# Chunked attention and a phase MLP on one core: zero products at the start, a token mix in three parts, and late transposes moved to DMA

## The chip, the cores and the metric

The kernel runs on one core of one Trainium2 chip. The core has TensorE (PE, matrix products; its weight loads are listed as PEld), VectorE (DVE), ScalarE (ACT), GpSimd (POOL) and SyncE (SP), which run at the same time and wait for each other by semaphores. DMA engines move data between HBM and SBUF and inside SBUF. The metric is the device time of one execution in microseconds (us), taken as the median of several runs. The span, a little shorter, is the time from the first to the last instruction in a profiled execution.

## What is computed

Inputs q, k, v have the shape (8 batches, 8 heads, 576 tokens, 64). Attention works inside chunks of 64 tokens; its result x (8, 576, 512) goes through a layer that turns each value by a phase, mixes the tokens and mixes the channels:

```python
# attention, per batch, head and chunk of 64 tokens
scores = scale * q_c @ k_c.T
attn = softmax(scores)
x = attn @ v_c                       # heads laid side by side: (8, 576, 512)
# phase layer
theta = x @ w_theta
zr, zi = x * cos(theta), x * sin(theta)
y = w_tok_r @ zr + w_tok_i @ zi      # over the 576 tokens of a batch
u = x + y
out = u + max(u @ w_ch, 0)           # (8, 576, 512), float32
```

## The kernel before

The batches are taken in four pairs (0 to 3). The 2 x 576 tokens of a pair are nine tiles of 128 rows, numbered 0 to 8: tiles 0 to 3 belong to the first batch, 5 to 8 to the second, and tile 4, the middle tile, holds the last 64 tokens of both. For attention the tiles form five groups: A (0, 1), B (2, 3), M (4), C (5, 6), D (7, 8).

The whole program is a list of steps in ORDER. A step such as `Y.31.1` is a kind (Y), a pair (3), a tile or group (1), and for TensorE's steps a number of the PSUM buffer. Each engine does its own steps in the order of the list. The start and the end of the list before:

```python
ORDER = """
lw.00 init.00 cw.00 q.0B TW.00.0 q.0A q.0M k.0B k.0A twd.00 T.0B.1 tk.0B lt.00 twa.00
T.0A.2 tq.0B tk.0A tq.0A S.0B.1 k.0M v.0A v.0M v.0B e.0B S.0A.0 e.0A T.0M.2 tq.0M tk.0M
new.00 q.0D q.1M S.0M.1 lw.01 V0.0A.2 e.0M V0.0M.0 v0.0A v0.0M q.0C V1.0M.1 v1.0M
V1.0A.2 X.0M.0 k.1M v1.0A k.0D k.0C V1.0B.1 v.0D q.1A v1.0B X.0A.2 lc.00 x.0M H.0M.0
V0.0B.1 x.0A q.2M v0.0B g.0M H.0A.2 X.0B.1 z.0M TW.01.0 twd.01 x.0B new.10 H.0B.1 v.1M
g.0A z.0A TW.02.2 twd.02 g.0B twa.01 z.0B T.0D.1 twa.02 tq.0D T.0C.0 T.1M.2 tk.1M Y.02.0
... cut ...
H.3C.1 U.30.0 u.30 W.28.1 w.28 W.30.0 w.30 W.31.1 w.31 g.3C z.3C W.32.0 Y.33.1 w.32 y.33
Y.37.0 Y.34.1 y.37 y.34 U.37.0 u.37 U.33.1 u.33 U.34.0 W.37.1 w.37 u.34 Y.36.0 W.34.1
y.36 w.34 W.33.0 w.33 Y.35.1 y.35 U.36.0 U.35.1 u.36 W.36.0 u.35 w.36 Y.38.1 y.38 W.35.0
U.38.1 w.35 u.38 W.38.0 w.38
""".split()
```

The kinds, as far as they matter here: q, k, v load inputs (issued by GpSimd, cast to 16 bit on the way); lw, lt, lc load the weights and cw casts one of them; TW turns the token weights on TensorE, twd and twa copy them out of PSUM on DVE and ACT; T, tq, tk turn q and k; S, e, V0, V1, v0, v1 are attention (scores, exponential, product with v, division). Then follow, for a group or a tile:

```python
    # X, x: x turned by TensorE, copied out by ACT
    def x_t(p, g, slot):
        j0, bb, s0 = GROUPS[g]
        n = 1 if bb is None else 2
        ps = psum2("ps_xT", slot, FP16)
        psv = ps.rearrange("p (r x) -> p r x", r=2)[:, :, 0 : n * NDB * CH]
        psv = psv.rearrange("p r (a c) -> p r a c", c=CH)
        for j in range(n):
            for db in range(NDB):
                for r in range(2):
                    nc.tensor.transpose(
                        psv[:, r, j * NDB + db, :],
                        st[p]["x"][half[r], j0 + j, db * P : db * P + P],
                        id16[half[r], half[r]],
                    )
        st[p]["ps_xT", g] = psv
    def x_copy(p, g):
        n = 1 if g == "M" else 2
        psv = st[p].pop(("ps_xT", g))
        xT = tmp.tile([P, 2 * NDB, P], FP16, name="xT")
        st[p]["xT", g] = xT
        nc.scalar.copy(
            out=xT[:, 0 : n * NDB].rearrange("p a (r c) -> p r a c", r=2), in_=psv
        )

    # H: theta = x @ w_theta (8 products for two tiles); g: cos and sin on ACT
    # z: zr and zi; the middle tile's halves for the other batch's rows move by DMA
    def phase(p, g):
        j0, bb, s0 = GROUPS[g]
        cos, sin = st[p].pop(("trig", g))
        x, zr, zi = st[p]["x"], st[p]["zr"], st[p]["zi"]
        if bb is not None:
            nc.vector.tensor_mul(zr[:, j0 : j0 + 2], x[:, j0 : j0 + 2], cos)
            nc.vector.tensor_mul(zi[:, j0 : j0 + 2], x[:, j0 : j0 + 2], sin)
            return
        lo, hi = half
        t = tmp.tile([P, DM], FP16, name="zmid")
        nc.vector.tensor_mul(t[lo], x[lo, j0], sin[lo, 0])
        nc.vector.tensor_mul(t[hi], x[hi, j0], cos[hi, 0])
        nc.sync.dma_start(zr[hi, j0], t[lo])
        nc.sync.dma_start(zi[lo, j0], t[hi])
        nc.vector.tensor_mul(zr[lo, j0], x[lo, j0], cos[lo, 0])
        nc.vector.tensor_mul(zi[hi, j0], x[hi, j0], sin[hi, 0])

    # Y: token mix of one tile, nine products (middle tile: two of half width each)
    def y(p, j, slot):
        s = st[p]
        ps = psum1("ps_y", slot)

        if j == MID:
            parts = [(half[bb], slice(KT * P, S), bb) for bb in range(2)]
        else:
            bb = int(j > MID)
            jl = j - bb * (MID + 1)
            parts = [(slice(0, P), slice(jl * P, jl * P + P), bb)]
        for i in range(2 * KT + 1):
            for rows, cols, bb in parts:
                if i == 0:
                    z, jz, kt = s["zi"] if bb else s["zr"], MID, 2 * KT
                else:
                    kt = i - 1
                    z = s["zr"] if kt < KT else s["zi"]
                    jz = bb * (MID + 1) + kt % KT
                nc.tensor.matmul(
                    ps[rows], wT[:, kt, cols], z[:, jz, :],
                    start=(i == 0), stop=(i == 2 * KT),
                )
        s["ps_y", j] = ps

    # y: u = x + y
    def add_x(p, j):
        u = tmp.tile([P, DM], FP16, name="u16", bufs=6)
        st[p]["u", j] = u
        nc.vector.tensor_tensor(
            out=u, in0=st[p].pop(("ps_y", j)), in1=st[p]["x"][:, j], op=ALU.add
        )

    # U, u: u turned by TensorE, copied out by DVE or ACT
    def u_t(p, j, slot):
        u = st[p]["u", j]
        ps = psum1("ps_uT", slot, FP16)
        psv = ps[:, 0:DM]
        for db in range(NDB):
            nc.tensor.transpose(
                psv[:, db * P : db * P + P], u[:, db * P : db * P + P], id16
            )
        st[p]["ps_uT", j] = psv

    def u_copy(p, j):
        uT = tmp.tile([P, DM], FP16, name="uT", bufs=4)
        st[p]["uT", j] = uT
        psv = st[p].pop(("ps_uT", j))
        if j % 2:
            nc.vector.tensor_copy(out=uT, in_=psv)
        else:
            nc.scalar.copy(out=uT, in_=psv)

    # W: u @ w_ch, four products; w: the last add, and the stores
    def w(p, j, slot):
        uT = st[p].pop(("uT", j))
        ps = psum1("ps_uw", slot)
        for db in range(NDB):
            nc.tensor.matmul(
                ps, uT[:, db * P : db * P + P], wch16[:, db, :],
                start=(db == 0), stop=(db == NDB - 1),
            )
        st[p]["ps_uw", j] = ps
    def relu_add(p, j):
        u = st[p].pop(("u", j))
        o = outp.tile([P, DM], FP32, name="o32")
        nc.vector.scalar_tensor_tensor(
            out=o, in0=st[p].pop(("ps_uw", j)), scalar=0.0, in1=u, op0=ALU.max, op1=ALU.add
        )
        if j == MID:
            to = [out[2 * p + b, KT * P : S, :] for b in range(2)]
        else:
            bb = int(j > MID)
            jl = j - bb * (MID + 1)
            s0 = (jl // 2) * GT + (jl % 2) * CH
            to = [out[2 * p + bb, s0 + r * P : s0 + r * P + CH, :] for r in range(2)]
        for r in range(2):
            nc.sync.dma_start(to[r], o[half[r]])
```

PSUM has buffers of two sizes, "wide" (three are used, by T, S, V, X, H, TW) and "thin" (two, by Y, U, W).

Of the kernel before, what the change touches and what calls it, by code (L numbers as in the profile page):

```python
# [18 lines left out]
lw.00 init.00 cw.00 q.0B TW.00.0 q.0A q.0M k.0B k.0A twd.00 T.0B.1 tk.0B lt.00 twa.00  # L19
T.0A.2 tq.0B tk.0A tq.0A S.0B.1 k.0M v.0A v.0M v.0B e.0B S.0A.0 e.0A T.0M.2 tq.0M tk.0M  # L20
new.00 q.0D q.1M S.0M.1 lw.01 V0.0A.2 e.0M V0.0M.0 v0.0A v0.0M q.0C V1.0M.1 v1.0M
V1.0A.2 X.0M.0 k.1M v1.0A k.0D k.0C V1.0B.1 v.0D q.1A v1.0B X.0A.2 lc.00 x.0M H.0M.0
V0.0B.1 x.0A q.2M v0.0B g.0M H.0A.2 X.0B.1 z.0M TW.01.0 twd.01 x.0B new.10 H.0B.1 v.1M
g.0A z.0A TW.02.2 twd.02 g.0B twa.01 z.0B T.0D.1 twa.02 tq.0D T.0C.0 T.1M.2 tk.1M Y.02.0
tk.0D S.0D.1 tq.1M q.1D S.1M.2 tk.0C y.02 e.0D Y.00.1 tq.0C k.1A y.00 Y.01.0 y.01 e.1M
U.00.1 v.0C V0.0D.0 v0.0D V1.0D.1 u.00 V0.1M.2 U.02.0 v1.0D W.00.1 v0.1M S.0C.0 w.00
q.1B X.0D.1 u.02 V1.1M.2 W.02.0 w.02 x.0D v1.1M H.0D.1 U.01.1 e.0C V0.0C.0 V1.0C.2 v0.0C
Y.03.0 k.1D v1.0C g.0D q.1C X.0C.0 T.1A.2 u.01 T.1D.1 x.0C y.03 tq.1A tq.1D k.1B v.1B
H.0C.0 U.03.1 tk.1D W.01.0 v.1C z.0D tk.1A X.1M.1 u.03 W.03.1 w.01 g.0C k.1C S.1D.2 z.0C
T.1B.0 tq.1B k.2M w.03 q.2B x.1M e.1D S.1A.1 Y.05.0 y.05 v.1A e.1A tk.1B Y.06.1 T.1C.2  # L30
S.1B.1 q.2D T.2M.0 q.2A y.06 tq.1C v.1D Y.08.0 tk.2M U.05.1 tk.1C e.1B tq.2M V0.1A.2
u.05 S.2M.0 e.2M y.08 S.1C.1 W.05.1 V1.1B.0 q.2C v0.1A U.08.0 v1.1B H.1M.2 e.1C V0.1B.1
V1.1A.0 u.08 v1.1A v0.1B w.05 Y.04.0 g.1M q.3C v.2M V1.1C.0 X.1B.1 y.04 v1.1C V0.1C.2
U.06.1 v0.1C Y.07.0 y.07 u.06 U.04.1 V0.1D.0 k.2D v0.1D V1.1D.2 x.1B v1.1D X.1A.1 W.08.0
k.2C w.08 v.2B H.1B.0 v.3M u.04 U.07.1 u.07 x.1A new.20 W.06.0 w.06 k.2B v.3C W.04.1
V0.2M.1 g.1B X.1C.2 x.1C X.1D.0 W.07.0 w.04 w.07 q.3A H.1A.2 k.2A v0.2M x.1D H.1D.0 z.1M
z.1B q.3D H.1C.1 v.3B g.1A T.2D.2 g.1D V1.2M.0 z.1A Y.10.1 Y.11.0 tq.2D tk.2D v1.2M g.1C
y.10 U.10.1 z.1D X.2M.2 T.2B.0 S.2D.1 v.2D y.11 z.1C x.2M tq.2B T.2A.2 Y.13.0 tk.2B
tq.2A y.13 H.2M.0 v.2C q.3M k.3C u.10 U.11.1 tk.2A u.11 W.10.0 w.10 g.2M e.2D z.2M
Y.15.1 T.2C.2 tk.2C S.2B.0 y.15 e.2B tq.2C V0.2D.1 v.2A v0.2D Y.12.0 y.12 U.15.1 S.2A.2  # L40
e.2A u.15 S.2C.1 V1.2D.0 U.13.0 v.3A u.13 e.2C W.11.1 Y.16.0 V1.2A.2 V0.2A.1 w.11 v1.2D
X.2D.0 U.12.1 y.16 u.12 W.13.0 W.15.1 v1.2A w.13 U.16.0 x.2D v0.2A H.2D.2 w.15 v.3D
W.12.1 w.12 V1.2B.0 V0.2C.1 u.16 v0.2C g.2D v1.2B Y.14.0 y.14 k.3A V1.2C.1 X.2A.0 x.2A
v1.2C V0.2B.2 Y.18.1 U.14.0 v0.2B T.3A.1 z.2D u.14 X.2C.0 X.2B.2 y.18 W.16.0 w.16 x.2C
H.2A.0 Y.17.1 y.17 x.2B tq.3A H.2C.2 W.14.0 k.3D g.2A U.17.1 g.2C w.14 H.2B.0 k.3M u.17
z.2C W.17.0 q.3B k.3B tk.3A T.3M.2 w.17 tk.3M S.3A.1 g.2B U.18.1 Y.27.0 tq.3M z.2B
T.3C.0 e.3A T.3D.2 V0.3A.1 y.27 z.2A u.18 W.18.0 tk.3C tq.3C new.30 w.18 Y.25.1 S.3M.0
tq.3D tk.3D v0.3A e.3M S.3D.2 e.3D T.3B.1 y.25 V1.3A.0 U.27.0 v1.3A u.27 tq.3B tk.3B
Y.26.1 y.26 W.27.0 U.25.1 S.3B.2 V1.3M.0 V0.3M.1 w.27 u.25 v1.3M Y.24.0 X.3A.0 v0.3M
e.3B y.24 V1.3B.2 V1.3D.1 U.26.1 Y.22.0 y.22 u.26 W.26.1 w.26 x.3A Y.21.0 X.3M.0 v1.3B  # L50
y.21 V0.3B.2 W.25.1 x.3M U.22.0 v1.3D H.3M.0 u.22 Y.23.0 v0.3B w.25 g.3M y.23 Y.20.1
U.23.0 S.3C.1 X.3B.2 x.3B V0.3D.0 u.23 W.22.0 y.20 w.22 W.23.1 U.20.0 H.3B.2 e.3C z.3M
v0.3D lw.00 H.3A.1 u.20 w.23 g.3B U.21.0 u.21 g.3A W.20.1 w.20 Y.28.0 z.3B y.28 U.24.1
z.3A V1.3C.0 X.3D.2 V0.3C.1 u.24 U.28.0 u.28 W.24.1 w.24 W.21.0 v1.3C v0.3C w.21 x.3D
Y.31.1 X.3C.2 y.31 H.3D.0 U.31.0 g.3D u.31 x.3C Y.32.1 y.32 Y.30.0 U.32.1 z.3D y.30 u.32
H.3C.1 U.30.0 u.30 W.28.1 w.28 W.30.0 w.30 W.31.1 w.31 g.3C z.3C W.32.0 Y.33.1 w.32 y.33
Y.37.0 Y.34.1 y.37 y.34 U.37.0 u.37 U.33.1 u.33 U.34.0 W.37.1 w.37 u.34 Y.36.0 W.34.1
y.36 w.34 W.33.0 w.33 Y.35.1 y.35 U.36.0 U.35.1 u.36 W.36.0 u.35 w.36 Y.38.1 y.38 W.35.0
U.38.1 w.35 u.38 W.38.0 w.38
# [4 lines left out]
def kernel(  # L64
# [35 lines left out]
    VP = D + 2  # L100
    half = [slice(0, CH), slice(CH, P)]
# [27 lines left out]
    wnat = glob.tile([P, KT + 1, 2, S], FP16, name="wnat")  # L129
    wraw = pairp.tile([P, KT, S], FP32, name="wraw")  # L130
    wend = glob.tile([CH, S], FP32, name="wend")
    v16 = glob.tile([P, 2 * NT, H, VP], FP16, name="v16")

    def setup():
        make_identity(nc, id16)
        nc.vector.memset(pihalf, math.pi / 2.0)
        nc.vector.memset(v16[:, :, :, D : D + 1], 1.0)
# [267 lines left out]

    def y(p, j, slot):
        s = st[p]
        ps = psum1("ps_y", slot)  # L410

# [143 lines left out]
```

The softmax here doesn't subtract the row's maximum and nothing guards it: scores larger than these inputs give would overflow.

## Time and profile before

| | before |
|---|---|
| device time, median of 3 runs | 221.02 us (220.84 to 221.03) |
| span of the profiled execution | 216.8 us |
| TensorE busy | 189.2 us (87%), 2898 products |
| DVE busy | 126.6 us (58%) |
| ACT busy | 119.0 us (55%) |
| GpSimd busy (issuing the input loads) | 104.3 us (48%) |

A line of the profile names the line of the kernel (L426), the engine, the operation and the tiles that it writes and reads. In a line of waits, the engine and line that waited stand first, then what it waited for, the time in total, how often, and the longest. In the chain of what ended last, each piece has a start, a length and what ran, or what was waited for. GpSimd's issues are the input loads: they run from 1.4 us to about 117 us, after that the DMA engines carry only the output stores and the small moves of the middle tile.

### The profile page before, as it was taken

To read this page: it belongs to the slowest core of one execution; us is meant where nothing else is said; L and a number is where in the kernel's file an instruction comes from. 1 tells how busy PE (TensorE), PEld (TensorE's weight loads), DVE (VectorE), ACT (ScalarE), POOL (GpSimd) and SP (SyncE) were. 2 spreads that over 40 slices of the span, in tenths; PEclk is the share of its full clock that TensorE was granted. 3 is DMA by queue.
4 is the path that set the end of the run, shared out by engine and by line. 5 is a ranking of instruction groups with operands and counts; after the bars stand their busy time and mean duration, and the time that the engine had idled before them with its cause. 6 is when DMAs were issued, how large, how long until landed. Compare 5 with 4: busy or idle time off the path is not lost.

```text
span 216.8 us, 6577 instructions
## 1 busy us (share of the span) xinstructions
PE 189.2 (87%) x2898; PEld 101.0 (47%) x2898; DVE 126.6 (58%) x248; ACT 119.0 (55%) x133; POOL 104.3 (48%) x130
## 2 busy tenths in 40 slices
PE   0354798999999999759999999989999999998881
PEld 0243445554555554426554554555455454444430
DVE  0024546576856876818776936877465794564541
ACT  2435359837895657844947476943266945501110
POOL 8998888799999899869982000000000000000000
PEclk9999999999999999999999999999999999999998
DMA  6999999999999999999999420322040772080534
GB/s 200 179 166 157 161 162 166 176 146 181 182 184 187 154 182 186 235 163 152 155 176 205 116 51 19 81 53 49 5 92 16 205 238 62 3 194 0 120 74 97
DMA packets 121819, 28.90 MB, mean 133 GB/s; under 512 B 113920, under 2 KB 116032, under 8 KB 121792
## 3 DMA queue, kind: packets, MB, share of 16 engines
q0 software_dynamic: 114176, 15.88, 112.1%
q1 hardware_dynamic: 7616, 12.62, 21.7%
q8 instruction: 22, 0.36, 0.7%
q14 instruction: 5, 0.04, 0.1%
HBM read 34.39 MB, written 9.44 MB: 202 GB/s over the span
## 4 chain that ended last, share of the span: by engine, by line
PE 70%; ACT 8%; DMA 7%; POOL 6%; DVE 5%; issue 1%; POOLq 0%; ACTq 0%
PE ps_y L426 30%; PE ps_uw L462 13%; PE ps_theta L365 13%; POOL qk L160 5%; PE ps_uT L444 4%; DMA v<-in_v_dram 4%; DMA zr<-zmid 3%; PE ps_x L309 3%; PE ps_xT L340 2%; PE ps_qkT L245 2%; PE ps_sT L276 2%; ACT cos L381 2%; DVE x L322 2%; ACT sin L385 2%; ACT kT L263 1%
## 5 line engine op out<-in xcount | busy, mean ns | idle before, releaser
L426 PEld LDWEIGHTS <-wT 128*128 128x128 f16 (+1 forms) x360 | 30.9, 100 | 38.2 <-DMA zr<-zmid 3.5
L426 PE MATMUL ps_y<-zr,wT 128*128 128x512 f16 (+1 forms) x180 | 41.4, 380 | 3.4 <-DMA zr<-zmid 3.4
L426 PE MATMUL ps_y<-zi,wT 128*128 128x512 f16 (+1 forms) x180 | 44.3, 380 | 0.0
L435 DVE TENSOR_TENSOR u<-ps_y,x 128x512 f16<-128x512 f32 x36 | 24.8, 690 | 30.2 <-PE ps_y L426 29.9
L462 PE MATMUL ps_uw<-wch,uT 128*128 128x512 f16 x144 | 35.9, 380 | 0.9 <-ACT uT L456 0.7
L365 PE MATMUL ps_theta<-wtheta,xT 128*128 128x512 f16 x144 | 36.3, 399 | 0.3 <-ACT xT L352 0.3
L168 POOL DMA_DIRECT2D v<-in_v_dram x40 | 34.1, 876 | 4.7 <-DMA v<-in_v_dram 1.5
L160 POOL DMA_DIRECT2D qk<-in_k_dram x40 | 34.1, 886 | 3.3 <-DMA qk<-in_k_dram 0.8
L160 POOL DMA_DIRECT2D qk<-in_q_dram x40 | 34.3, 885 | 1.7 <-issue 0.6
L471 DVE SCALAR_TENSOR_TENSOR o<-ps_uw,u 128x512 f32<-128x512 f32 x36 | 24.8, 688 | 17.0 <-PE ps_uw L462 17.0
L456 ACT COPY uT<-ps_uT 128x512 f16<-128x512 f16 x20 | 11.7, 586 | 35.3 <-PE ps_uT L444 35.3
L352 ACT COPY xT<-ps_xT 128x1024 f16<-128x1024 f16 (+1 forms) x20 | 18.4, 930 | 21.3 <-PE ps_xT L340 21.2
L322 DVE TENSOR_TENSOR x<-ps_x,recip 128x512 f16<-128x512 f32 (+1 forms) x40 | 25.5, 638 | 1.4
L381 ACT ACTIVATE cos<-ps_theta,pihalf 128x1024 f16<-128x1024 f32 (+1 forms) x20 | 20.6, 1031 | 10.3 <-PE ps_theta L365 5.8
L263 ACT COPY kT<-ps_qkT 128x1024 f16<-128x1024 f16 x16 | 16.0, 1016 | 13.9 <-DVE qT L263 9.2
L365 PEld LDWEIGHTS <-xT 128*128 128x128 f16 x144 | 13.9, 101 | 16.5 <-issue 2.6
L289 ACT ACTIVATE eT<-ps_sT 128x1024 f16<-128x1024 f32 (+1 forms) x20 | 18.4, 939 | 4.2 <-PE ps_sT L276 4.0
L462 PEld LDWEIGHTS <-uT 128*128 128x128 f16 x144 | 12.7, 98 | 14.0 <-ACT uT L456 1.2
L385 ACT ACTIVATE sin<-ps_theta 128x1024 f16<-128x1024 f32 (+1 forms) x20 | 18.7, 936 | 0.0
L245 PE MATMUL ps_qkT<-id,qk 64*128 64x64 f16 x576 | 13.1, 197 | 2.8 <-DMA qk<-in_k_dram 2.0
L444 PE MATMUL ps_uT<-id,u 128*128 128x128 f16 x144 | 14.0, 220 | 1.1 <-DVE u L435 1.0
L263 DVE COPY qT<-ps_qkT 128x1024 f16<-128x1024 f16 x16 | 10.8, 686 | 5.4 <-ACT kT L263 4.7
(40 smaller groups left out, 151.6 us busy)
## 6 DMA issues: line engine op xcount, KB each, us to landing
out_dram<-o SPq DMA_DIRECT2D x72, 128.0 KB, 2.9
qk<-in_q_dram POOLq DMA_DIRECT2D x32, 128.0 KB, 6.5
qk<-in_k_dram POOLq DMA_DIRECT2D x32, 128.0 KB, 6.2
v<-in_v_dram POOLq DMA_DIRECT2D x32, 128.0 KB, 6.5
wraw<-in_moe_w_tok_r_dram SPq DMA_DIRECT2D x2, 1152.0 KB, 6.3
wnat<-in_moe_w_tok_i_dram POOLq DMA_DIRECT2D x1, 576.0 KB, 6.6
qk<-in_q_dram POOLq DMA_DIRECT2D x8, 64.0 KB, 6.3
wtheta<-in_moe_w_theta_dram POOLq DMA_DIRECT2D x1, 512.0 KB, 7.1
```

Source lines behind the costliest of these rows:

```text
L160: nc.gpsimd.dma_start(nats[p, g][rows, which, r], (q, k)[which][b, :, t0 : t0 + n, :].rearrange("h s d -> s h d"),)
L168: nc.gpsimd.dma_start(v16[rows, slot + r, :, 0:D], v[b, :, t0 : t0 + n, :].rearrange("h s d -> s h d"),)
L263: copy(out=t.rearrange(flat), in_=ps.rearrange(flat))
L322: nc.vector.tensor_tensor(out=st[p]["x"][:, j0 : j0 + n, f * NE * D : (f + 1) * NE * D].rearrange("p c (h d) -> p c h d", h=NE), in0=psv[: ...
L365: nc.tensor.matmul(ps[:, j * DM : j * DM + DM], xT[:, j * NDB + db, :], wtheta16[:, db, :], start=(db == 0), stop=(db == NDB - 1),)
L381: nc.scalar.activation(out=cos[:, 0:n].rearrange("p a e -> p (a e)"), in_=pin, func=AF.Sin, bias=pihalf, scale=1.0,)
L385: nc.scalar.activation(out=sin[:, 0:n].rearrange("p a e -> p (a e)"), in_=pin, func=AF.Sin)
L426: nc.tensor.matmul(ps[rows], wT[:, kt, cols], z[:, jz, :], start=(i == 0), stop=(i == 2 * KT),)
L435: nc.vector.tensor_tensor(out=u, in0=st[p].pop(("ps_y", j)), in1=st[p]["x"][:, j], op=ALU.add)
L444: nc.tensor.transpose(psv[:, db * P : db * P + P], u[:, db * P : db * P + P], id16)
L462: nc.tensor.matmul(ps, uT[:, db * P : db * P + P], wch16[:, db, :], start=(db == 0), stop=(db == NDB - 1),)
L471: nc.vector.scalar_tensor_tensor(out=o, in0=st[p].pop(("ps_uw", j)), scalar=0.0, in1=u, op0=ALU.max, op1=ALU.add)
```

## The change

The kernel after computes the same. Its differences:

1. **Products of zeros.** A new tile `blank` of zeros is filled at the start, and fourteen steps D are put between TensorE's first steps. Each is two products of 128x512 whose result nobody reads. They are there to keep the array active while it waits for its first inputs.
2. **The first token mix in three parts.** For the first four tiles of pair 0, Y is cut into Ya (products 0 and 1: zr of group A), Yb (4 and 5: zi of group A) and Yc (the rest), so that it can begin before all of z is there.
3. **The middle tile last.** Each Y now ends with the products of the middle tile instead of beginning with them, and the DMA that moves its halves is a step of its own (zm), apart from z.
4. **Late u and x by DMA transposes.** For the five groups of pair 3, and for twenty tiles of pairs 1 to 3, X and x, or U and u, give way to one DMA transpose (Xd, Ud), issued by SyncE, which writes the turned tile straight to SBUF.
5. **The store as a step of its own** (st), apart from the last add, so that the order of the DMAs on SyncE's queue can be chosen.
6. **A new order** of all steps, with group M first at the start. A second load of a token weight (lw.00), near the end of the old list and read by nothing, is gone.

The diff, cut to its core (of the ORDER list the start, the places of the first transposes, and the end):

```diff
-lw.00 init.00 cw.00 q.0B TW.00.0 q.0A q.0M k.0B k.0A twd.00 T.0B.1 tk.0B lt.00 twa.00
... cut ...
+ones.00 D.00.0 lw.00 cw.00 D.00.1 init.00 D.00.0 D.00.1 q.0M q.0B q.0A D.00.0 k.0M
+D.00.1 D.00.0 D.00.1 k.0B TW.00.0 twa.00 k.0A D.00.0 T.0M.1 tk.0M D.00.1 D.00.0 tq.0M
+S.0M.2 e.0M lt.00 T.0B.1 T.0A.2 tk.0A tq.0B D.00.1 tq.0A tk.0B S.0A.2 v.0M V1.0M.1 v.0A
+e.0A D.00.0 V0.0M.2 twd.00 S.0B.0 new.00 v1.0M V1.0A.1 v0.0M V0.0A.2 v0.0A v.0B q.1M
+v1.0A lw.01 X.0M.2 e.0B V1.0B.0 X.0A.1 v1.0B x.0M H.0M.2 V0.0B.0 x.0A v0.0B q.0C k.1M
+v.0C H.0A.1 g.0M X.0B.0 z.0M zm.0M x.0B g.0A TW.02.2 H.0B.0 T.1M.1 twa.02 twd.02 TW.01.2
+z.0A Ya.01.1 tk.1M tq.1M g.0B Ya.03.0 twd.01 S.1M.1 k.0C q.0D z.0B q.1B twa.01 Yb.01
+T.0C.0 e.1M Yb.03 tq.0C Yc.03 tk.0C S.0C.2 Yc.01 v.1M y.03 k.0D Ya.02.0 e.0C lc.00
+V1.0C.1 new.10 V0.0C.0 Yb.02 y.01 v0.0C Yc.02 v.0D v1.0C U.01.1 X.0C.2 u.01 T.0D.0
+V0.1M.1 Ya.00.1 Yb.00 x.0C tk.0D y.02 U.02.0 tq.0D v0.1M V1.1M.2 k.1B v1.1M S.0D.1
... cut ...
+x.2C tk.3A tq.3A S.2A.1 S.3A.0 y.14 Ud.17 U.12.1 u.12 Y.18.0 y.18 e.2A Y.16.1 k.3M y.16
+e.2B W.17.0 v.2A H.2C.1 e.3A w.17 V1.2A.2 v1.2A V0.2A.0 W.12.1 st.04 zm.2M Y.15.0 v0.2A
+Ud.14 v.3D w.12 y.15 g.2C V1.2B.2 v1.2B V0.2B.0 v0.2B q.3B X.2A.1 W.14.1 x.2A Ud.18 w.14
+st.17 U.16.0 u.16 T.3C.2 X.2B.1 W.16.0 w.16 tk.3C U.15.1 x.2B H.2A.0 u.15 q.3D k.3B
... cut ...
+V0.3A.1 T.3B.0 Y.26.1 Y.20.0 tq.3B st.18 v0.3A tk.3B Ud.28 V1.3A.0 y.26 e.3M y.20 v1.3A
+V1.3M.2 V1.3C.1 v1.3M v1.3C Y.24.1 V0.3C.0 T.3D.2 st.15 Ud.27 S.3B.1 y.24 tq.3D v0.3C
+Ud.26 W.26.0 w.26 e.3B W.27.1 v.3B w.27 tk.3D V1.3B.1 V0.3B.0 v0.3B v1.3B S.3D.2 Ud.20
+st.27 W.28.0 w.28 Y.21.1 y.21 Xd.3A Ud.21 Y.25.0 V0.3M.0 st.28 v0.3M y.25 e.3D V1.3D.2
+V0.3D.1 st.26 Xd.3M Y.22.1 H.3A.0 Ud.24 v0.3D y.22 v1.3D W.21.0 w.21 W.20.1 H.3M.1 g.3A
+Y.23.0 Ud.22 w.20 y.23 W.22.1 g.3M Xd.3B st.21 z.3M st.20 H.3B.2 Ud.25 g.3B Xd.3D W.24.0
+w.22 w.24 W.25.1 H.3D.0 w.25 Xd.3C z.3B H.3C.1 z.3A g.3C Ud.23 W.23.0 st.22 w.23 z.3C
+g.3D zm.3M Y.32.1 y.32 Y.31.0 z.3D Y.30.1 y.31 Y.37.0 st.24 st.25 y.30 st.23 Ud.30 y.37
+Y.35.1 W.30.0 y.35 Ud.31 W.31.1 w.30 Ud.32 Ud.35 Ud.37 w.31 st.30 st.31 Y.36.0 W.35.1
+y.36 w.35 W.32.0 w.32 st.35 Ud.36 Y.34.1 y.34 Y.33.0 W.37.1 y.33 W.36.0 w.37 Y.38.1
+st.32 Ud.34 w.36 Ud.33 y.38 st.37 W.34.0 w.34 W.33.1 w.33 st.36 st.34 st.33 U.38.0 u.38
+W.38.1 w.38 st.38 D.00.0
... cut ...
+    blank = const.tile([P, DM], FP16, name="blank")
+    def fill():
+        nc.vector.memset(blank, 0.0)
... cut ...
+    def idle(p, i, slot):
+        ps = psum1("ps_idle", slot)
+        for r in range(2):
+            nc.tensor.matmul(ps, blank[:, 0:P], blank, start=True, stop=True)
... cut ...
+    def x_dma(p, g):
+        j0, bb, s0 = GROUPS[g]
+        n = 1 if bb is None else 2
+        xT = tmp.tile([P, 2 * NDB, P], FP16, name="xT")
+        st[p]["xT", g] = xT
+        nc.sync.dma_start_transpose(
+            xT[:, 0 : n * NDB], st[p]["x"][:, j0 : j0 + n].rearrange("p a e -> p (a e)")
+        )
... cut ...
-        nc.sync.dma_start(zr[hi, j0], t[lo])
-        nc.sync.dma_start(zi[lo, j0], t[hi])
+        st[p]["zmid"] = t
         nc.vector.tensor_mul(zr[lo, j0], x[lo, j0], cos[lo, 0])
         nc.vector.tensor_mul(zi[hi, j0], x[hi, j0], sin[hi, 0])
-
-
-    def y(p, j, slot):
+    def mid_move(p, g):
+        lo, hi = half
+        t = st[p].pop("zmid")
+        nc.sync.dma_start(st[p]["zr"][hi, MID], t[lo])
+        nc.sync.dma_start(st[p]["zi"][lo, MID], t[hi])
+    def y(p, j, slot=None, ks=range(2 * KT + 1)):
         s = st[p]
-        ps = psum1("ps_y", slot)
+        if ks[0] == 0:
+            s["ps_y", j] = psum2("ps_y2", slot) if (p, j) in WIDE_Y else psum1("ps_y", slot)
+        ps = s["ps_y", j][:, 0:DM]
         if j == MID:
             parts = [(half[bb], slice(KT * P, S), bb) for bb in range(2)]
... cut ...
             bb = int(j > MID)
             jl = j - bb * (MID + 1)
             parts = [(slice(0, P), slice(jl * P, jl * P + P), bb)]
-        for i in range(2 * KT + 1):
+        for kt in ks:
             for rows, cols, bb in parts:
-                if i == 0:
-                    z, jz, kt = s["zi"] if bb else s["zr"], MID, 2 * KT
+                if kt == 2 * KT:
+                    z, jz = s["zi"] if bb else s["zr"], MID
                 else:
-                    kt = i - 1
                     z = s["zr"] if kt < KT else s["zi"]
                     jz = bb * (MID + 1) + kt % KT
                 nc.tensor.matmul(
                     ps[rows], wT[:, kt, cols], z[:, jz, :],
-                    start=(i == 0), stop=(i == 2 * KT),
+                    start=(kt == 0), stop=(kt == 2 * KT),
                 )
-        s["ps_y", j] = ps
... cut ...
+    def u_dma(p, j):
+        uT = tmp.tile([P, DM], FP16, name="uT", bufs=4)
+        st[p]["uT", j] = uT
+        nc.sync.dma_start_transpose(uT.rearrange("p (a c) -> p a c", a=NDB), st[p]["u", j])
... cut ...
+        st[p]["o", j] = o
+
+    def store(p, j):
+        o = st[p].pop(("o", j))
... cut ...
+        "Ya": lambda p, j, slot: y(p, j, slot, range(0, 2)),
+        "Yb": lambda p, j: y(p, j, None, range(4, 6)),
+        "Yc": lambda p, j: y(p, j, None, (2, 3, 6, 7, 8)),
```

## The prediction

> **What bounds the kernel now.** I first read the page's slices, then the chain that ended last, TensorE's waits, and last the groups. Between 39 and 195 us TensorE is almost never idle:
>
> ```profile
> 38.87:86.00 47.13, 46.62 (x885) 25.23 (x885) 32.06 (x66) 34.05 (x38) 44.60 (x54) 1.00 2.25 175
> 86.00:95.00 9.00, 5.63 (x63) 2.79 (x62) 5.45 (x12) 6.89 (x7) 6.85 (x8) 1.00 2.02 212
> 95.00:195.00 100.00, 99.38 (x1396) 51.84 (x1395) 66.78 (x126) 56.66 (x64) 18.51 (x22) 1.00 0.81 105
> 195.00:212.10 17.10, 15.12 (x91) 6.96 (x87) 7.79 (x14) 1.76 (x3) 0.00 (x0) 1.00 0.30 65
> ```
>
> These are stretches of the span: after its length come the busy times of PE, weight loads, DVE, ACT and POOL. The reader is to see one hole in TensorE (3.4 us at 86 to 95) and a thin tail (2.0 us), and that DVE, ACT and, after 120 us, the DMA engines have room.
>
> The chain gives the real pace, because a busy TensorE is not TensorE at its peak. Its pieces (start, length, what):
>
> ```profile
> 15.03 7.59 DMA v<-in_v_dram
> ...
> 25.78 1.82 PE ps_theta L365 x4
> ...
> 27.96 3.35 PE ps_theta L365 x8
> ...
> 33.12 1.85 PE ps_theta L365 x8
> ...
> 38.87 2.05 PE ps_y L426 x9
> ...
> 86.89 7.50 DMA zr<-zmid
> 94.43 4.06 PE ps_y L426 x18
> ...
> 212.09 0.69 DVE o L471
> ```
>
> A 128x512 product costs 455 and 419 ns apiece at 26 to 31 us (1.82/4, 3.35/8), but 231 ns at 33 us and 216 ns in the steady pieces (1.94 us for nine). So the first twelve theta products run at half pace.
>
> From the chain I took a length for each step in the steady part: Y 1.94 us, W 0.865, H 1.73 (middle group 0.865), U 0.22, T 0.57 (0.34), S 0.38 (0.22), V 0.25 (0.15), X 0.34 (0.22), TW 1.47. Times their counts in the order list (36, 36, 16+4, 36, 16+4, 16+4, 32+8, 16+4, 3) they sum to **177.4 us** of TensorE work in a span of 216.8. The other 39.4 us are the prize: 24.0 before the first token mix (it starts at 38.87 with 14.9 us of work done), 10.7 between there and 212.1 (173.2 passed, 162.5 worked), and 4.7 for the last add and store.
>
> TensorE's waits name the two large holes:
>
> ```profile
> PE ps_wT L211 <- ACT wnat L184: 9.0, 1, 9.0
> PE ps_y L426 <- DMA zr<-zmid: 3.4, 1, 3.4
> ```
>
> **What the Trainium skill says.** "TensorE: Matmul & The Clock Gate", Part 1: the array starts at half clock, goes to full after one busy window of about 3.4 us, and falls back after an idle one. The trace agrees in size (about 427 ns, then 216). Its summary line shows a granted clock of 1.00 in the slow stretch too, so that column doesn't show this gate. "DMA: Bandwidth & Descriptors", section DMA Transpose (X-bar): a transposing DMA takes 2-byte types, writes SBUF and is issued from the sync or scalar queue. No run here has one yet. The same page, Anatomy of one DMA, gives about 2 us fixed for a transfer, and its Latency section 261 GB/s for a transposing DMA. The trace agrees with the first where the queues are quiet:
>
> ```profile
> L401 SPq DMA_DIRECT2D zr<-zmid x4: 482/518/596, 29.8 to 168.3; - x4
> ...
> DMA to landing us min/median/max: 2.0/5.6/7.5
> ```
>
> That is the middle tile's 64 KB move inside SBUF: half a microsecond of SyncE's time each, landed in 2.0 us at best, 7.5 us under the input loads.
>
> **Part 1, products of zeros.** Fourteen D steps of two products each are added: 28 x 0.427 = 12 us cold, 6 us warm. TensorE's start has 24 us in which it does no useful work, because loads and casts are awaited, so I count them as free. What they can save is the cold excess of the twelve theta products, (1.82 - 0.86) + (3.35 - 1.73) = 2.6 us, plus perhaps 0.5 us in the small steps around. But between the scores of group A and the arrival of v the list has only two D steps, and v is still awaited at 22 us (chain: the v load lands at 22.6). TensorE may fall back to cold just before theta. I count 60%: **-1.6 us**.
>
> **Part 2, new head and the split token mix.** Loads, not TensorE, set the time of the first theta: the bytes up to v of group B are the same 2432 KB before and after, only reordered with the middle group first. So theta of M begins near 25 us as before. What changes is the stretch after it. Before, all three groups' trig (ACT 2.0 us each for A and B) and the weight copies end before the first Y at 38.87. Afterwards Ya needs only group A's zr and the first wT, Yb group A's zi, and Yc the rest. I follow ACT: x of A ends about 26.1, table load 1.28, trig of M 1.28, copy of x of B 1.0, trig of A 2.1, which is about 31.8; a wT copy, zi and TW.01 bring Ya to about 34.5. There the list has 13.7 us of work behind it, so idle time in the head is about 20.8 instead of 24.0: **-3.2 us**, which includes the -1.6 of part 1. The 3.5 us of Ya and Yb then cover trig of B.
>
> **Part 3, U and X by DMA.** Off TensorE: 20 U x 0.22 = 4.4 and five X, 4 x 0.34 + 0.22 = 1.6, together **-6.0 us**, nearly all in stretches where TensorE is gapless, so worth its full length. The order's sum falls to 171.4. ACT also loses about ten uT copies (586 ns) and five xT copies (930 ns), DVE ten of 421 ns; neither is the bound, so I count nothing.
>
> **Part 4, the middle tile last.** Before, each Y began with the middle tile, which waits for the move of zmid; now it comes last (8 x 216 ns = 1.7 us later), and the move's issue is a step of its own that the order can place early. The hole of 3.4 us should go: **-3.4 us**. Tile 38's own end (u, U, copy, W, add, store) stays; the tail of 4.7 us too.
>
> **Part 5, what the transposes cost.** They share SyncE's in-order queue with 72 stores (about 0.55 us of issue each, 1.1 per tile). No row shows a transposing issue. I choose 1.5 us for a 128x512 tile, about three plain issues, and 2.3 for a pair of tiles, and land them 2.0 + 128 KB/261 GB/s, about 2.5 us, after issue (estimate from the skill's page and the 2.0 above). In the dense stretch, from Ud.28 to Ud.23, SyncE then has 9 x 1.5 + 4 x 2.3 + 1.5 + 6 stores x 1.1 = 31 us of issue, against 28 us of TensorE work by my lengths. So it falls about 3 us behind at X of D and C. In the end stretch (tiles 30 to 37) the list leaves 3 to 5 us between an add and its W, against about 4 needed: another 0.5 to 1 us. I count **+3 us**, and +0.5 for Ud.17, .14 and .18, which may still meet the last loads (landing up to 7.5 us).
>
> **Sum.** 216.8 - 3.2 - 6.0 - 3.4 + 3.5 = 207.7. The thin end of before (2.0 us lost between 195 and 212) is filled by more W steps after the last Y: -0.7. Span 207.0. The timed median is 4.2 us above the profiled span before; I keep that: about **211 us**.
>
> **Rivals.**
> First, *SyncE becomes the bound*. If a tile's transpose takes 2.5 to 3 us of the queue instead of 1.5, the dense stretch holds 18 tile units x 2.75 + 6.6 = 56 us against 28, and TensorE waits more than 25 us there: 230 us or more, slower. For it: 29 tile units on one queue that also carries every store, and no transposing DMA in the old trace to vouch for the size. Against it: the order keeps 5 to 6 us between most issues and their users, as if the latency were known, and does not put the last tile through it.
> Second, *the loads hold the head*. The head is set by the v loads and then by ACT's trig; if so, zeros and split bring only 1 us instead of 3.2: 213 us. For it: the 7.59 us of v in the chain. Against it: the gap from theta (26) to Y (39) is not load time.
> Third, *the new order is simply as good as drawn*: the transposes are wholly hidden, TensorE stays warm throughout, and some of the remaining 7 us of small waits between 39 and 195 go as well: 205 us.
>
> **Range and chances.** The third rival gives 205, my sum 211, the second 213; a queue at 2 us a tile gives about 217. The range 205 to 218 holds these. Faster by over 2% means below 216.6; only the first rival, or two of the others together, breaks it: 0.78. Within 2%: 0.12. Slower: 0.10.
>
> **What would show it.** In the changed profile: theta products at 216 ns spacing before 31 us (part 1; if near 427, the zeros failed); the first split Y near 34 to 35 us instead of 38.87 (part 2); U at x16 and X at x15 steps, 64 products of 128x128 for U (part 3); no wait of Y for zmid over 1 us (part 4); waits of W for a DMA of uT, and of theta for a DMA of xT, of some 3 us together (part 5). The prediction is wrong if those last waits exceed 8 us, or if the transposes' time to landing is above 6 us after 120 us.

## The result, and the profile after

The changed kernel takes 213.26 us (213.03 to 213.72) against 220.93 us for the kernel before: a ratio of 0.967, 95% interval 0.963 to 0.971. In a second measurement, among the experiments below, the ratio was 0.962 (0.960 to 0.965). The span of the profiled execution fell from 216.8 to 210.7 us.

The page's slices of the changed kernel, one digit for 5.3 us: TensorE's busy share, and the clock it was granted, in tenths.

```profile
PE   7678698897989999999999999999899988999981
PEclk9965579999999999999999999999999999999999
```

TensorE is busy from the first microseconds, with zeros; but its clock is down in the slices from 11 to 32 us, the stretch for which the zeros were meant. (Thirteen of the fourteen D steps stand in the head; the last one ends the list, behind the last W.) Now stretches of the span, in the columns of before (length, then busy time of PE, weight loads, DVE, ACT, POOL, then the clock):

```profile
40.00:50.00 10.00, 7.87 (x190) 4.48 (x188) 5.75 (x13) 4.95 (x6) 8.29 (x10) 1.00 2.22 165
...
80.00:100.00 20.00, 20.00 (x363) 10.39 (x360) 13.86 (x26) 15.27 (x17) 17.76 (x22) 1.00 2.29 177
...
170.00:180.00 10.00, 8.43 (x39) 3.52 (x38) 5.99 (x11) 3.79 (x4) 0.00 (x0) 1.00 0.71 143
```

The hole at 86 to 95 us is gone. Two new ones are there: 2.1 us at 40 to 50, and 1.6 us at 170 to 180. The chain that ended last (start, length, what) says what the second is, and how the head went:

```profile
25.54 1.82 PE ps_theta L388 x4
...
27.72 2.69 PE ps_theta L388 x8
...
30.79 1.01 ACT xT L366
31.80 1.02 ACT cos L404
32.82 0.91 ACT sin L408
...
166.02 3.09 DMA xT<-x
169.11 0.05 issue
169.15 1.92 PE ps_theta L388 x8
...
171.23 3.25 DMA xT<-x
174.48 0.05 issue
174.53 3.63 PE ps_theta L388 x16
...
205.93 0.69 DVE o L506
```

The first four theta products still take 455 ns apiece, as before. At 171 us, with theta of D and C due, the transpose of x stands on the path; the 3.25 us of that piece are not all lost, since TensorE has two W to do meanwhile. The first part of the first token mix starts at 36.71 us in the timeline (38.87 before).

TensorE's waits in the changed kernel (who waited, for what, total, times, longest):

```profile
PE ps_sT L290 <- DVE recip L335: 1.3, 1, 1.3
...
PE ps_theta L388 <- DMA xT<-x: 1.0, 1, 1.0
PE ps_x L323 <- ACT eT L303: 0.9, 1, 0.9
...
PE ps_sT L290 <- ACT kT L277: 0.8, 1, 0.8
PE ps_qkT L259 <- ACT sin L408: 0.8, 1, 0.8
...
PE ps_uw L497 <- DMA uT<-u: 0.5, 1, 0.5
```

And of the weight loads, between 155 and 182 us:

```profile
PEld L388 <- DMA xT<-x: 2.1, 2, 1.5
...
PEld L497 <- DMA uT<-u: 1.0, 1, 1.0
```

No wait for zmid is left. For transposes the products wait 1.5 us in all and the weight loads in front of them, which read the turned tile, 3.1 here and 0.3 later. The other waits shown are for DVE and ACT, all but one of them at 40 to 62 us. What a transpose of u (128x512) costs stands in the view of its tile: SyncE's time for an issue in ns (min/median/max), then the time to landing.

```profile
L482 SPq DMA_TRANSPOSE uT<-u x20: 1188/1213/2321, 114.6 to 199.9; - x20
...
DMA to landing us min/median/max: 2.4/2.4/6.6
```

And for x (128x1024, group M 128x512):

```profile
L375 SPq DMA_TRANSPOSE xT<-x x5: 1243/1282/1922, 156.1 to 172.6; - x5
...
DMA to landing us min/median/max: 2.5/3.2/3.8
```

### The profile page after: what moved, and what is told of

Read it like the earlier page. It is cut to its first block, busy times and chain, and to the rows that moved or that the text cites. A ratio compares the mean times of both kernels' runs of the same rounds, so it can differ in the third digit from the quotient of the medians.

```text
span 210.7 us, 6370 instructions
## 1 busy us (share of the span) xinstructions
PE 191.4 (91%) x2774; PEld 96.7 (46%) x2774; DVE 123.6 (59%) x240; ACT 111.3 (53%) x119; POOL 104.4 (50%) x130
## 4 chain that ended last, share of the span: by engine, by line
PE 65%; DVE 9%; ACT 9%; DMA 7%; POOL 6%; issue 1%; SPq 0%; POOLq 0%; ACTq 0%
PE ps_y L457 27%; PE ps_theta L388 14%; PE ps_uw L497 13%; POOL qk L174 5%; DMA v<-in_v_dram 4%; PE ps_x L323 3%; DMA xT<-x 3%; ACT kT L277 3%; PE ps_qkT L259 3%; PE ps_sT L290 2%; DVE qT L277 2%; PE ps_xT L354 2%; DVE x L336 2%; ACT xT L366 1%; PE ps_uT L474 1%
## 5 line engine op out<-in xcount | busy, mean ns | idle before, releaser
L457 PE MATMUL ps_y<-zr,wT 128*128 128x512 f16 (+1 forms) x180 | 44.4, 381 | 0.0
L457 PE MATMUL ps_y<-zi,wT 128*128 128x512 f16 (+1 forms) x180 | 42.0, 379 | 0.0
L388 PEld LDWEIGHTS <-xT 128*128 128x128 f16 x144 | 13.7, 100 | 17.9 <-issue 2.1
L366 ACT COPY xT<-ps_xT 128x1024 f16<-128x1024 f16 (+1 forms) x15 | 13.9, 931 | 12.2 <-PE ps_xT L354 12.1
L491 ACT COPY uT<-ps_uT 128x512 f16<-128x512 f16 x9 | 5.3, 592 | 24.3 <-PE ps_uT L474 24.2
L335 DVE RECIPROCAL recip<-ps_x 128x8 f32<-128x8 f32 (+1 forms) x40 | 7.9, 197 | 10.5 <-PE ps_x L323 10.2
```

The lines of the kernel that those rows point to most:

```text
L388: nc.tensor.matmul(ps[:, j * DM : j * DM + DM], xT[:, j * NDB + db, :], wtheta16[:, db, :], start=(db == 0), stop=(db == NDB - 1),)
L457: nc.tensor.matmul(ps[rows], wT[:, kt, cols], z[:, jz, :], start=(kt == 0), stop=(kt == 2 * KT),)
```

## The experiments

Each gives its ratio to the kernel before, measured on the same chip with 95% interval; differences of a per cent between experiments are read from these ratios. A time is the median of all executions; a ratio leaves out those in which the chip was in a slower state, so the two can differ by some tenths of a per cent.

**No zeros.**

```diff
-ones.00 D.00.0 lw.00 cw.00 D.00.1 init.00 D.00.0 D.00.1 q.0M ...
+ones.00 lw.00 cw.00 init.00 q.0M ...          (all fourteen D left out)
```

> The changed kernel without its fourteen steps of zero products; all else as it is. My theory: the zeros keep the array at full clock only until about 12 us, it is back at half clock before the first theta, and all they bring is the end of the second theta (2.69 us for eight products instead of about 3.4). Then this runs 0.3 to 1.0 us slower than the changed kernel (213.3 us), about 214.0, and theta of group M takes 1.8 us with and without. Rival: the zeros are what the head gains, 2.5 us or more: 215.8 or above.

Measured: 213.28 us, ratio 0.973 (0.965 to 0.980), not to be told from the changed kernel's 0.967 (0.963 to 0.971). The middle ratios differ by 1.3 us, so the trace has to decide. The timeline of this kernel (start, length, line, operation):

```profile
25.64 1.89 PE L385 MATMUL ps_theta<-wtheta,xT 128*128 128x512 f16 x4
27.83 2.29 PE L385 MATMUL ps_theta<-wtheta,xT 128*128 128x512 f16 x8
```

Theta of M takes the same as with zeros, and theta of A 2.29 us, less than the 2.75 us with them. The eight profiles of kernels that have exactly the fourteen D steps bear this out: theta of M takes 1.89 us in every one, and theta of A between 1.90 and 3.32 us, so the moment at which the clock rises varies from one to the next. The first mix starts at 36.42 us without zeros, at 36.71 with them. The span is 0.8 us longer here (211.5), but behind the head: the products' waits for transposes are 2.5 us instead of 1.5. As written, the zeros bring nothing to the head. The rival falls, and so does the half of my theory by which they speed up theta of A.

**More zeros**, in the gaps that were left.

```diff
+D.00.1   (ahead of T.0M)
+D.00.0   (ahead of S.0A)
+D.00.1   (ahead of V1.0A)
+D.00.0   (ahead of X.0M)
```

> The changed kernel with four more steps of zero products, in the gaps that TensorE still had between 11 and 24 us (before T of M, S of A, V1 of A, X of M). My theory: if the array stays at full clock, the first twelve theta products take 2.6 us instead of 4.5, trig of A begins up to 1.9 us earlier, and the end moves by 1 to 1.9 us: 211.5 to 212.3 us. Rival 1: small products and transposes of 64 columns do not keep the clock up, it stays at half: no gain or 0.5 us lost to the added products. Rival 2: the clock rises, but ACT's chain of copies and trig sets the head anyway: theta at 216 ns and the time unchanged within 0.4 us.

Measured: 212.23 us, ratio 0.968 (0.960 to 0.976). Its timeline:

```profile
26.34 1.04 PE L386 MATMUL ps_theta<-wtheta,xT 128*128 128x512 f16 x4
27.56 1.90 PE L386 MATMUL ps_theta<-wtheta,xT 128*128 128x512 f16 x8
...
35.76 1.04 PE L455 MATMUL ps_y<-zr,wT 128*128 128x512 f16 x4
```

Here both run at full pace (1.90 us for eight); rival 1 falls. The clock was not held throughout: it was at 0.52 from 10 to 12 us and at about 0.58 from 20 to 24 us, but back at 1.00 before the first theta. Theta starts 0.9 us later here, after a wait of 1.4 us for v, and the first mix is 0.95 us earlier than in the changed kernel. Since the unaltered kernel's own first mix lay at 36.71 and at 36.18 us in two profiles, and the intervals overlap, the gain in time is not shown. The pace is: theta of M ran at full pace in both kernels with the four more steps (this one and the last one below), and at half in all eight with the fourteen alone.

**The middle tile last, alone, in the kernel before.**

```diff
-        for i in range(2 * KT + 1):     # i = 0: the middle tile
+        for kt in range(2 * KT + 1):    # kt = 2 * KT, at the end: the middle tile
```

> The kernel before with one edit: each token mix ends with the middle tile's product instead of beginning with it. Order, moves and all else as before. My theory: the hole of 3.4 us at 91 to 94 us shrinks by the eight products that now come first, 1.7 us, and what is left of it is a wait in the middle of the mix; 1.5 to 2 us faster than before. If the hole were gone altogether: 3.4 us faster. Rival: what ends the hole is trig and phase of groups A and D, which end at 95 us by the profile, not the move: no change.

Measured: 218.0 us, ratio 0.989 (0.987 to 0.992), so 2.4 us faster (1.8 to 3.0). Its waits:

```profile
PE ps_y L423 <- DMA zr<-zmid: 1.9, 1, 1.9
```

The hole of 3.4 shrinks by about the eight products that now come first; the move still took 7.88 us in its chain. The rival (trig sets the end of the hole) falls.

**The middle tile first again, in the changed kernel.**

```diff
-    def y(p, j, slot=None, ks=range(2 * KT + 1)):
+    def y(p, j, slot=None, ks=(8, 0, 1, 2, 3, 4, 5, 6, 7)):
-        "Yc": lambda p, j: y(p, j, None, (2, 3, 6, 7, 8)),
+        "Yc": lambda p, j: y(p, j, None, (8, 2, 3, 6, 7)),
```

> The changed kernel with the middle tile's product first again in every whole token mix (and first of the last part in the split ones); its move stays a step of its own, early in the order. My theory: in the new order the move lands well before its first reader in pairs 0 to 2, and only in pair 3, where it is issued at 176.6 us and the first mix starts at 179.0, is it waited for: 1 to 2 us slower than the changed kernel. Rival 1: no difference, because the early step alone removed the hole. Rival 2: 3.4 us slower, the whole hole of the kernel before.

> The changed kernel unaltered, on the same chip as the next two, so that differences of one per cent can be read. Both theories: 212.5 to 214 us.

Measured: 215.06 us, ratio 0.974 (0.970 to 0.979), against 211.94 us and 0.962 (0.960 to 0.965) for the unaltered kernel on the same chip: some 3 us slower. Its waits have one for the move, in pair 3 as expected:

```profile
PE ps_y L455 <- DMA zr<-zmid: 0.9, 1, 0.9
```

With its weight load that wait is 1.39 us in the timeline. By the ratios the kernel is 2.7 us slower, more than the 1 to 2 that I expected and nearer to rival 2. In the two profiles part of the difference is not the edit's. This is theta of A, in this kernel and in the unaltered one:

```profile
27.65 3.32 PE L386 MATMUL ps_theta<-wtheta,xT 128*128 128x512 f16 x8
...
27.53 2.36 PE L388 MATMUL ps_theta<-wtheta,xT 128*128 128x512 f16 x8
```

Here it ran longer at half pace, which the edit doesn't touch, and the first mix starts at 37.27 instead of 36.18 us. That is 1.1 of the 2.2 us by which the spans of these two executions differ (212.4 and 210.2); the wait in pair 3 is the rest. It does not settle the times: the mean granted clock of the other five executions, 0.962 to 0.973, is no lower than the unaltered kernel's, 0.960 to 0.972. The place of the wait is shown; what else makes up the 3 us stays open.

**The transposes alone, in the kernel before.**

```diff
-... y.31 H.3D.0 U.31.0 g.3D u.31 ...
+... y.31 Ud.31 H.3D.0 g.3D ...           (likewise for all twenty; Xd in the place of X)
```

> The kernel before with the same twenty u and five x turned by DMA transposes, each issued right after u (or at the place of X), stores where they were; nothing else changed. 6.0 us of TensorE work go. My theory: in the old order W follows 2 to 4 us after its u, where the transpose needs 0.7 + 1.2 + 2.4 us from the end of Y, more if others stand ahead of it on SyncE; so waits of 4 to 8 us appear and the time is 218 to 223 us against 220.5. Rival: the old order hides them too: 214.5 to 216.

Measured: 222.2 us, ratio 1.004 (1.001 to 1.008): slightly slower than before, with 6.0 us less work on TensorE. Its waits:

```profile
PE ps_theta L372 <- DMA xT<-x: 4.0, 3, 2.1
PE ps_y L433 <- DMA zr<-zmid: 4.0, 1, 4.0
PE ps_uw L474 <- DMA uT<-u: 2.5, 3, 1.2
```

6.5 us of waits for the two transposes take the place of the work removed. (The wait for zmid, 3.4 us before, is 4.0 here, and the granted clock averages 0.95 from 95 to 130 us; together these may cost another 2 us.) In its chain the stretch from the end of an add to the W behind it is 2.41 to 2.72 us of DMA three times over: W comes too soon. My expectation had counted the 1.2 us of the issue twice; the 2.4 us to landing contain it.

**All transposes back on TensorE, in the new order.**

```diff
-... Xd.3A Ud.21 Y.25.0 ...
+... X.3A.0 x.3A Uw.21.1 u.21 Y.25.0 ...  (Uw: U with a wide PSUM buffer)
```

> The changed kernel with all twenty-five DMA transposes taken back to TensorE, with a copy on ACT or DVE, at the same places of its order (a place later where u or x is only just being made); for u a wide PSUM buffer is used so that no thin one is waited for. My theory: 6.0 us of TensorE work come back, some 2 us of waiting for SyncE between 160 and 180 us go, and the copies after X of C and D are waited for, 1 to 2 us: 217 to 219 us, which is 4 to 6 slower than the changed kernel. Rival: SyncE's queue costs as much as the transposes save: within 1 us of 213.3.

Measured: 239.68 us, ratio 1.088 (1.075 to 1.101): 26 us slower than the changed kernel, where I had expected 4 to 6. Theory and rival are both wrong, by far.

**Only u back on TensorE,** to take the wide buffers out of it.

```diff
-... st.23 Ud.30 y.37 Y.35.1 W.30.0 ...
+... st.23 U.30.1 u.30 y.37 Y.35.1 W.30.0 ...   (likewise for all twenty; thin buffers)
```

> The changed kernel with the twenty u turned on TensorE again and copied out by DVE or ACT, in the two thin PSUM buffers that Y and W use; x of pair 3 stays a DMA transpose. My theory: 4.4 us of TensorE work come back, a few waits for a thin buffer or a copy are added (1 to 3 us, above all where four or five U follow each other at the end), and the 2 us of waiting for SyncE go: 216 to 219 us against 213.3. Rival: the transposes gave nothing net: within 1 us of 213.3. If it is above 225, the new order itself, not the work taken off TensorE, is what the transposes make possible.

Measured: 238.64 us, ratio 1.080 (1.073 to 1.086). So the wide buffers were not the cause. A piece of its timeline; the brackets give the idle time before and what ended it:

```profile
128.42 0.59 ACT L490 COPY uT<-ps_uT 128x512 f16<-128x512 f16 x1 [5.29 <-PE ps_uT L473]
...
129.02 1.28 ACT L403 ACT_TABLE_LOAD   x1
...
130.31 1.11 ACT L403 ACTIVATE cos<-ps_theta,pihalf 128x1024 f16<-128x1024 f32 x1
131.33 1.02 ACT L407 ACTIVATE sin<-ps_theta 128x1024 f16<-128x1024 f32 x1
132.39 0.41 PE L353 MATMUL ps_xT<-id,x 64*128 64x64 f16 x16 [3.69 <-ACT sin L407]
```

ACT sits idle for 5.29 us in front of the copy of one u, because TensorE has not reached its U. Cos and sin, whose theta was done at 124.8 us, stand behind that copy in ACT's queue. When they are through, TensorE has waited 3.69 us for the PSUM buffer that they read. One copy of 0.59 us thus held up ACT for 5.29 us and TensorE for 3.69. And the hole costs more than its length, for the clock falls after it. The same four products of W before and after:

```profile
125.12 1.04 PE L496 MATMUL ps_uw<-wch,uT 128*128 128x512 f16 x4
...
137.09 1.89 PE L496 MATMUL ps_uw<-wch,uT 128*128 128x512 f16 x4
```

**The same, with the copies on DVE.**

```diff
-        if j % 2:
+        if j % 2 or late:        # late: the twenty tiles
             nc.vector.tensor_copy(out=uT, in_=psv)
```

> The kernel with the twenty u turned on TensorE in the new order (238.6 us), with the copies of those u all on DVE instead of every second one on ACT. My theory: half of its loss is that ACT, which works in order, stands at a copy that waits for TensorE while exponentials and trig are due behind it; off ACT, that part goes: 226 to 232 us. Rival 1: the loss is TensorE waiting in order for u, for the copies and for the thin buffers, on whichever engine they are: 236 us or more. Rival 2: all of it is ACT: below 222 us.

Measured: 230.81 us, ratio 1.050 (1.042 to 1.058): 7.8 us of the 25 go when ACT has none of these copies. That bears out the theory for a third of the loss, not half. The traces tell what goes and what stays. The clock, with half the copies on ACT and with none:

```profile
PEclk9857699999999999999999769989999999997999
...
PEclk9857589999999999999999999999999999999999
```

After the head the clock falls three times in the first and never in the second, and the same 2854 products keep TensorE busy for 203.1 us in the first and 198.7 in the second. The mean clock says the same of all their executions: 0.934 to 0.949 against 0.955 to 0.963. TensorE's waits for sin and for the exponential were 7.5 us and are 1.4. Its waits for copies of u stay. These are W and U, first with half the copies on ACT, then with all on DVE (busy time and mean ns of one, then the idle time before them and what ended most of it):

```profile
L496 PE MATMUL ps_uw<-wch,uT 128*128 128x512 f16 x144 | 37.2, 389 | 5.7 <-ACT uT L490 3.5
...
L473 PE MATMUL ps_uT<-id,u 128*128 128x128 f16 x144 | 14.7, 227 | 3.8 <-ACT uT L490 2.1
...
L497 PE MATMUL ps_uw<-wch,uT 128*128 128x512 f16 x144 | 36.3, 380 | 7.5 <-DVE uT L489 7.1
...
L473 PE MATMUL ps_uT<-id,u 128*128 128x128 f16 x144 | 14.0, 219 | 4.2 <-DVE uT L489 2.8
```

With Y's waits for a PSUM buffer that such a copy frees, TensorE waits 10.6 us for these copies in the first kernel and 11.8 in the second, against 0.7 us for all copies of u in the changed kernel. So of the 17.8 us by which this kernel's span is longer than the changed kernel's, 4.4 are the work of U and about 11 are waits for its copies, which is what rival 1 named. The 7.9 us by which the span with half the copies on ACT is longer still go with the holes behind ACT and the slower clock after them.

**The first mixes whole.**

```diff
-... Ya.01.1 ... Ya.03.0 ... Yb.01 ... Yb.03 Yc.03 ... Yc.01 ...
+... Y.03.0 ... Y.01.1 ...               (each where its last part stood)
```

> The changed kernel with the first four token mixes whole again, each at the place where its last part stood. My theory: the parts fill TensorE's gaps between 36.7 and 44 us, 1.7 us of work each for Ya and Yb, but TensorE is waiting for ACT and DVE there in any case, so undoing it costs 1 to 2 us: 214.3 to 215.3. Rival 1: it costs all of 3.5 us. Rival 2: nothing, the stretch is set by copies and trig.

Measured: 215.45 us (213.72 to 216.49), ratio 0.974 (0.967 to 0.981), against 0.967 (0.963 to 0.971) for the changed kernel. The middle value, 1.5 us slower by the ratios, is what I expected; the intervals overlap. The profile is of the slowest of its four executions (216.49 us). There TensorE is busy for 7.05 us between 40 and 50 us, against 7.87 in the changed kernel, waits 2.0 us for DVE at the end of it, and the clock falls: theta at 51 us takes 2.96 us for eight products, 1.1 us more than at full pace. In this one profile, then, most of what the parts save is the clock.

**Stores from GpSimd.**

```diff
-            nc.sync.dma_start(to[r], o[half[r]])
+            (nc.gpsimd if p >= 2 else nc.sync).dma_start(to[r], o[half[r]])
```

> The changed kernel with the stores of pairs 2 and 3 issued by GpSimd, which has nothing to do after 117 us, instead of SyncE. My theory: SyncE's queue, 1.2 us a tile for stores among the transposes, is what theta and W wait for at 160 to 180 us (2 us lost); without the stores the transposes start earlier, those waits go, and the time falls by 1.5 to 2.5 us to 211 to 212. Rival: the waits are the transposes' own latency or come from elsewhere: no gain, or a longer tail if a store from GpSimd lands later.

Measured: 212.95 us, ratio 0.965 (0.959 to 0.971): no gain that can be seen. Yet in its profile the wait of theta for xT is down to 0.2 us and the mixes of pair 3 start at 177.1 instead of 178.9 us. The end of its timeline:

```profile
204.14 0.69 DVE L504 SCALAR_TENSOR_TENSOR o<-ps_uw,u 128x512 f32<-128x512 f32 x1 [1.25 <-PE ps_uw L495]
205.12 1.05 POOL L519 DMA_DIRECT2D out_dram<-o  x2 [0.56 <-DVE o L504]
```

The last add starts at 204.14 us, 1.8 us earlier than in the changed kernel (205.93), but the span ends at 211.0. From the end of the last add it is 6.2 us (211.0 - 204.83) against 4.1 (210.7 - 206.62). So the theory was right on the queue, and the second half of the rival on the tail: what was won is paid back after the last add.

**Both ideas, with the last stores on SyncE.**

```diff
+D.00.1, D.00.0, D.00.1, D.00.0          (as in "more zeros")
+            early = p == 2 or (p == 3 and j in (0, 1, 2, 5))
-            nc.sync.dma_start(to[r], o[half[r]])
+            (nc.gpsimd if early else nc.sync).dma_start(to[r], o[half[r]])
```

> The changed kernel with the four more steps of zero products and with the stores of pair 2 and of tiles 0, 1, 2 and 5 of pair 3 issued by GpSimd; the last five tiles' stores stay on SyncE. My theory: the two gains lie in different stretches (1.0 us in the head, 1.8 us of waiting for SyncE at 160 to 180 us) and add up, once the last stores no longer land later: 2.3 to 2.8 us faster than the changed kernel. Rival: a gain in the head is eaten by the copies and trig of ACT and DVE that the order meets at 40 to 60 us, and the loads end no earlier: 1 us or less.

Measured: 211.47 us, ratio 0.958 (0.955 to 0.962), span 208.1, against 211.94 us, 0.962 (0.960 to 0.965) and 210.2 for the changed kernel on the same chip. The span is 2.1 us shorter in the one profile of each; the intervals of the ratios overlap. I had expected 2.3 to 2.8 us; the times differ by 0.5 and the ratios by 0.9, as the rival had it. It is the fastest of all the versions, but that it beats the changed kernel is not shown.

## Why the prediction was right, step by step

The direction and the size came out: 211 us forecast, 213.3 measured. But two errors cancelled in part, and that 211 lies so near is to that extent luck. The forecast span was 207.0 us, the measured one 210.7. And I added 4.2 us from span to device time, having set the median of the timed runs against the span of one execution that itself took 218.63 us; the distance within one execution is 1.8 us there and 2.3 in the changed kernel (213.03 - 210.7). In the prediction's own terms, with its lengths per step:

| term | forecast | measured |
|---|---|---|
| TensorE's work, without zeros | 171.4 | 171.4 (same counts) |
| no useful work before the first mix | 20.8 | 36.7 - 13.7 = 23.0 |
| lost between there and the last W | 10.1 | (205.9 - 36.7) - 157.7 = 11.5 |
| from the last W to the end | 4.7 | 210.7 - 205.9 = 4.8 |

So the 6.1 us of the span are the 6.0 of work taken off TensorE and 1.0 in the head, less 0.9 lost elsewhere. In the third row the hole of 3.4 us is gone, but new waits outweigh it: about 2.4 us for transposes (part 5) and 1.7 us more idle time at 40 to 60 us than before (part 2).

**Part 1, the zeros (-1.6 us): wrong.** They bring nothing to theta. The doubt in the prediction, that TensorE falls back before theta, was right, and the weight given to it (40%) too small. Only when the gaps were filled as well did theta run at 216 ns. The 427 ns that I set beside the trace stands in no line of it, which have 455 and 419. I also wrote that the clock column doesn't show this gate: it does in the changed kernel (0.50 at 15 to 25 us). But the kernels without zeros show 1.00 at the start while products are spaced at half pace (455 ns in the kernel before), so in these traces a 1.00 ahead of the first change says nothing.

**Part 2, the head (-3.2 us in all): direction right, size too large.** It measured -1.0 (-1.5 in the second profile). The term that was mis-sized is trig of A. I had it end at 31.8 us, and it ended at 33.7: theta of A ended at 30.4, cold, and ACT's copy of x of B stood in front of it. So the first Ya came at 36.7, not 34.5. And part of what the split wins is lost right after it: 2.1 us of idle at 40 to 50 us, where the kernel before had 0.25:

```profile
40.00:50.00 10.00, 9.75 (x186) 5.16 (x184) 5.65 (x12) 6.54 (x9) 9.33 (x12) 1.00 2.24 154
```

The order now brings scores there before DVE and ACT are ready (the waits of ps_sT for 1.3 and 0.8 us above).

**Part 3, work off TensorE (-6.0): right in size, but it is not a gain on its own.** The four combinations, in us:

| | U on TensorE | U by DMA |
|---|---|---|
| old order | 220.5 | 222.2 (X by DMA too) |
| new order | 238.6 | 213.3 (X by DMA too) |

Neither the transposes nor the order gains alone. The right-hand column differs by whether the order leaves room between a Y and its W: 0.7 us for the add and 2.4 for the transpose, more when others stand ahead of it on SyncE. The lower left is no fair price for TensorE's transposes, since the places of U there follow a simple rule and weren't tuned; it shows that this order leans on the absence of U and its copies. The prediction counted nothing for those copies because neither engine was the bound. By the runs with u back on TensorE that was too quick: TensorE waits for them for some 11 us, they hold up what stands behind them, and the clock falls after the longer holes.

**Part 4, the middle tile (-3.4): right.** Its hole is gone from the trace. Alone in the old order the new product order gives 2.4 us and leaves a wait of 1.9; so the 3.4 needed the early issue, or the new order, too. Back in the new order, the middle tile first costs about 3 us by the times, of which the trace puts 0.9 to 1.4 down to the wait.

**Part 5, the transposes' cost (+3.5): mechanism right, size too large for the issue.** An issue took 1.21 and 1.28 us, not 1.5 and 2.3, and the whole way from the start of the issue to landing 2.4 and 3.2 us, where I had added 2.5 to the issue. (The fixed 2 us that I took from the Trainium skill, "DMA: Bandwidth & Descriptors", Anatomy of one DMA, are stated there for transfers that GpSimd issues; for SyncE only the 2.0 us of the trace stood behind them.) The stretch from 163.7 to 179.0 us holds 13.2 us of work by my lengths, so about 2.1 us are lost to SyncE's queue where I had 3; with the stores moved away 1.8 us of it came back. In the end stretch W's weight loads waited 0.3 us in all for a transpose, not 0.5 to 1. The sign named in advance, waits of some 3 us together, was met (3.4 us at the weight loads), and after 120 us no transpose took more than 3.8 us to land.

The first rival (SyncE as the bound, 230 us) is out: the queue kept up except at one place. The second (the loads and ACT hold the head: 1 us from zeros and split, 213 us) is what was measured in the head, and its time was nearer than mine. The third would have needed a warm array and hidden transposes; it had neither.

## What to carry to other kernels

Work taken off the bounding engine is a gain only if its replacement's latency fits between producer and user (in the old order it didn't, and 6.0 us less work gave nothing), so ask first where the order leaves that room, and move the order and the work together. A copy on an engine that works in order can cost far more than its own length, through what stands behind it in the queue and through the engine that waits for it, even where the copying engine is half idle. A hole in TensorE can cost more than its length too: look at the pace of the products behind it. When warming an array with idle products, look at all the gaps up to the first real work: sixteen of the 28 products lay in the first seven microseconds, the gaps behind them stayed open, and nothing was won.

## What the runs showed of the hardware

A DMA transpose inside SBUF takes SyncE 1.21 us for 128x512 and 1.28 us in the median for 128x1024, so its issue hardly depends on size here, against about 0.55 us for a plain move. Counted from the start of the issue, it lands in 2.4 and 3.2 us (medians), and in 6.6 and 5.1 us for the first two, issued at 114.6 and 118.6 us, while the last input loads land. A store issued last by GpSimd ended the program 6.2 us after the last add, one issued by SyncE 4.1 us after it. Products of zeros raise the clock: in both kernels with more zeros, theta ran at full pace from its first product. And the length of a hole alone doesn't tell whether the clock falls after it: it fell after one of 3.69 us and one of 2.59 (u on TensorE) and one of 1.97 us (the first mixes whole), but not after the 3.4 us in the kernel before.
